# The first loads of a fused attention kernel: order of x and wkA, x's first chunk in two halves, the gate column, six warm-ups

## The chip, the cores and the metric

The kernel runs on one core of a Trainium2 chip. The metric is the device time of one execution in microseconds (us), measured over several executions; beside it there is one execution recorded by the hardware profiler, whose trace the profile lines in this document come from. TensorE (PE in the profile, with its weight loads as PEld) does the matrix products, VectorE (DVE) and ScalarE (ACT) the elementwise work, GpSimd (POOL) a few small copies. DMA transfers are issued from two queues, SyncE's (SP) and ScalarE's (ACT), and run on 16 shared DMA engines.

## The reference

Two linear-attention blocks, A and B, work on the same x (2048 rows of 640 values, bf16), with 32 heads of 20 values; a gate mixes their outputs row by row.

```python
g = sigmoid((x * gate_w).sum(-1, keepdims=True))
# for each of A and B:
q, k, v = split_heads(x @ wqkv)            # wqkv: 640 x 1920
phi = lambda t: where(t > 0, t + 1, exp(t)) + 1e-6
kv = einsum("bhsd,bhse->bhde", phi(k), v)
z = einsum("bhsd->bhd", phi(k))
num = einsum("bhqd,bhde->bhqe", phi(q), kv)
den = einsum("bhqd,bhd->bhq", phi(q), z)[..., None] + 1e-6
o = merge_heads(num / den) @ wo
out = g * o_A + (1 - g) * o_B
```

## The kernel before, in words

x is cut into 16 chunks of 128 rows, and the 640 features into 5 row blocks of 128 (DT = 5). A product with a weight needs x with features on the partitions (xT), while a load brings it with rows on the partitions (xn). For the first four chunks TensorE makes xT: `x_transpose` (L221) does five 128x128 transposes into PSUM, and VectorE copies them to xT, in two pieces where `cuts` says (0, 2, DT). The other twelve chunks are transposed on the way in by 15 DMA transposes on SP's queue (L137 to L141).

The program is one long TensorE stream. It begins with the warm-ups, matmuls on constants (L179), and the transposition of the gate vector into a column (L181 to L186): gate_w is loaded as a 5x128 tile `grow`, transposed by TensorE into the bank of the warm-ups, copied to `gsb` by VectorE, and written by five GpSimd copies into column 640 of wkA, one for each row block. The second half of every kA product is thus 321 columns wide (`k_mm`, L244), and its last column is the gate's logit.

Then `k_first` (L262) works through the first four chunks by hand, under a manual schedule, so that TensorE's order is the order of the code. Each chunk takes 10 matmuls, five row blocks by two halves of 320 columns, into one of four PSUM slots; the inner function `part(i, cs)` does the row blocks `cs` of chunk i. `k_done` (L251) hands a chunk to ACT (exp) and VectorE (two operations), which make phi(k). After it come the q blocks of the first 512 rows (`q_block`, L304), the other k chunks, and all later stages: the Gram products (`gs`, L380), the same for B, and the output stage. None of these is touched.

The loads of the first stage are issued in the order of the code, lines 125 to 141. Chunk q of the first 512 rows is made of the rows 4p + q, so that a load of one chunk (`load_x`) is 128 rows of 1,280 bytes; a row block of wkA (`load_wk`) is 128 rows of the same size. SP's queue issues x0, wkA's block 0, block 2, blocks 3 and 4 in one, then wqA in two loads, then the DMA transposes; ACT's queue issues the gate, x1, wkA's block 1, x2 and x3. Loads complete on eight semaphores taken in turn, so the ninth load waits, before it is issued, until the first has landed, and so on.

Of the kernel before, what the change touches and what calls it, by code (L numbers as in the profile page):

```python
# [8 lines left out]
P = 128  # L9
FP32 = mybir.dt.float32  # L10
BF16 = mybir.dt.bfloat16
# [3 lines left out]
S, D, H = 2048, 640, 32  # L15
Dh = D // H
DT = D // P
# [3 lines left out]
HB = 512  # L21
# [12 lines left out]
def kernel(  # L34
# [11 lines left out]
    nc = tc.nc  # L46
# [6 lines left out]
    work = ctx.enter_context(tc.tile_pool(name="work", bufs=2))  # L53
# [6 lines left out]
    def ps_raw(name, slot=None):  # L60

        if slot is None:
            slot = turn[0]
            turn[0] = (slot + 1) % 4
        return psum.tile([P, 4 * HB], BF16, tag=f"ps{slot}", name=name)

    def ps(name, slot=None):

        return ps_raw(name, slot).bitcast(FP32).rearrange("p (b n) -> p b n", b=2)

    xT = persist.tile([P, DT, S], BF16, name="xT")
    xn = persist.tile([P, ST, D], BF16, name="xn")
# [6 lines left out]
    ident = persist.tile([P, P], BF16, name="ident")  # L79
# [33 lines left out]
    xb0 = x2[0:CB * P, :].rearrange("(p q) d -> p q d", q=CB)  # L113
    wk = [None, None]
# [3 lines left out]
    def load_x(eng, lo, hi):  # L118
        eng.dma_start(out=xn[:, lo:hi, :], in_=xb0[:, lo:hi, :])

    def load_wk(eng, lo, hi):
        eng.dma_start(out=wk[0][:, lo:hi, 0:D], in_=wq_dram[0][:, lo:hi, D:2 * D])

    grow, logitT = R[0:DT, 0, 0, 0:P], R[0:2 * ST, 0, 1, 0:P]
    nc.scalar.dma_start(out=grow, in_=gate_w.rearrange("(c p) -> c p", p=P))
    load_x(nc.sync, 0, 1)
    load_x(nc.scalar, 1, 2)
    load_wk(nc.sync, 0, 1)
    load_wk(nc.scalar, 1, 2)
    load_wk(nc.sync, 2, 3)  # L130
    load_x(nc.scalar, 2, 3)
    load_wk(nc.sync, 3, DT)
    load_x(nc.scalar, 3, 4)
    wq[0] = wpool.tile([P, DT, D], BF16, tag="wq", name="wqA")
    for lo, hi in ((0, 2), (2, DT)):
        nc.sync.dma_start(out=wq[0][:, lo:hi, :], in_=wq_dram[0][:, lo:hi, 0:D])
    for n in range(1, NB):  # L137
        for c in range(DT):
            nc.sync.dma_start_transpose(
                out=xT[:, c, n * HB:(n + 1) * HB], in_=x2[n * HB:(n + 1) * HB, c * P:(c + 1) * P]  # L140
# [4 lines left out]
    for r in range(4):  # L145
        rows = slice(32 * r, 32 * r + 32)
        nc.gpsimd.tensor_copy(out=I4[rows], in_=ident[rows, rows])
    nc.gpsimd.tensor_copy(
        out=spread[:].rearrange("p (h t) -> p h t", t=TW), in_=I4[:, :, None].to_broadcast([P, H, TW])
    )  # L150
    nc.gpsimd.tensor_tensor(
        out=I16[0:2 * ST], in0=ident[0:2 * ST, 0:ST], in1=ident[0:2 * ST, ST:2 * ST], op=ALU.add
    )
    chosen = R[0:2 * ST, 1, 0:2, :].rearrange("p a (b n) -> p (a b) n", b=2)
    for h in range(2):
        for q in range(2):
            i0 = h * hc + q
            nc.gpsimd.tensor_copy(
                out=chosen[:, 2 * h + q, :].rearrange("p (j n) -> p j n", j=4),
                in_=I16[0:2 * ST, i0:i0 + hc - 1:2][:, :, None].to_broadcast([2 * ST, 4, 32]),  # L160
            )
    nc.gpsimd.memset(maskE[:], 1.0)
    for sign, base in ((1, 0), (-1, Dh - 1)):
        nc.gpsimd.affine_select(
            out=maskE[:], in_=maskE[:], pattern=[[-sign * Dh, WB[0] // Dh], [0, Dh]],
# [3 lines left out]
    for sign, base in ((1, 0), (-1, TW - 1)):  # L169
        nc.gpsimd.affine_select(  # L170
            out=headE[:], in_=headE[:], pattern=[[-sign * TW, H]],
# [4 lines left out]
    raw = ps_raw("warm", 3)  # L176
    warm = raw.bitcast(FP32).rearrange("p (b n) -> p b n", b=2)
    one_l, one_r = [nc.const_aps.tensor(1.0, [P, n], BF16) for n in (P, HB)]
    for k in range(7):  # L179
        nc.tensor.matmul(warm[:, 0, :], lhsT=one_l, rhs=one_r, start=True, stop=True)  # L180
    gcol = raw[:, 2 * HB:2 * HB + DT]  # L181
    nc.tensor.transpose(out=gcol, in_=grow, identity=ident[0:DT, 0:DT])
    gsb = work.tile([P, DT], BF16, tag="rT", name="gsb")
    nc.vector.tensor_copy(out=gsb[:], in_=gcol)
    for c in (0, 1, 2, 4, 3):
        nc.gpsimd.tensor_copy(out=wk[0][:, c, D:D + 1], in_=gsb[:, c:c + 1])  # L186

    def by_group(dst, lhsT, src, h):

        for c in range(DT):  # L190
            for j in range(4):
                r0 = h * 2 * HB + j * RB
                nc.tensor.matmul(
                    dst[32 * j:32 * j + 32, :], lhsT=lhsT[:, c, :], rhs=src[:, c, r0:r0 + RB],
                    start=(c == 0), stop=(c == DT - 1), tile_position=(0, 32 * j),
                )
# [24 lines left out]
    def x_transpose(i, slot, eng, cuts=(0, DT)):  # L221
        pt = ps_raw("xt", slot)
        for c in range(DT):
            nc.tensor.transpose(out=pt[:, c * P:(c + 1) * P], in_=xn[:, i, c * P:(c + 1) * P], identity=ident[:])
        copy = nc.scalar.copy if eng == "act" else nc.vector.tensor_copy
        src = pt[:, 0:D].rearrange("p (c n) -> p c n", c=DT)
        for lo, hi in zip(cuts, cuts[1:]):
            copy(out=xT[:, lo:hi, i * P:(i + 1) * P], in_=src[:, lo:hi])
# [15 lines left out]
    def k_mm(b, i, c, pt, hf):  # L244
        w = HF + (hf if b == 0 else 0)
        nc.tensor.matmul(  # L246
            pt[:, hf, 0:w], lhsT=xT[:, c, i * P:(i + 1) * P], rhs=wk[b][:, c, hf * HF:hf * HF + w],
            start=(c == 0), stop=(c == DT - 1),
        )

    def k_done(b, i, pt):  # L251
        side = (lambda: nc.scalar.copy(out=logit[:, i:i + 1], in_=pt[:, 1, HF:HF + 1])) if b == 0 else None
        phi(pk[:, i, :].rearrange("p (b n) -> p b n", b=2), pt[:, :, 0:HF], HF, side=side)

    def k_chunk(b, i, slot=None):
        pt = ps(f"k{'AB'[b]}", slot)
        for hf in range(2):
            for c in range(DT):
                k_mm(b, i, c, pt, hf)
        k_done(b, i, pt)  # L260

    def k_first():  # L262

        pts = [ps("kA", (2 + i) % 4) for i in (0, 1)]

        def part(i, cs):
            for c in cs:
                for hf in range(2):
                    k_mm(0, i, c, pts[i], hf)

        for i in range(2):
            x_transpose(i, i, "dve", (0, 2, DT))
        for i in range(2):
            part(i, (0, 1))
        for i in range(2):
            part(i, (2,))
        x_transpose(2, 0, "dve", (0, 2, DT))
        pts.append(ps("kA", 1))
        part(0, (3, 4))
        part(2, (0, 1, 2))  # L280
        x_transpose(3, 0, "dve")
        k_done(0, 0, pts[0])
        for i in (1, 2):
            part(i, (3, 4))
            k_done(0, i, pts[i])
        k_chunk(0, 3, 0)

    def mixed(t, m):

# [440 lines left out]
    with tc.manual_schedule():  # L730
        k_first()
# [9 lines left out]
    for n in range(1, NB):  # L741
        nc.sync.dma_start(
            out=xn[:, n * CB:(n + 1) * CB, :], in_=x2[n * HB:(n + 1) * HB, :].rearrange("(q p) d -> p q d", p=P)
# [8 lines left out]
    def bank(pool, name, n=1):  # L752
        return pool.tile([P, HB] if n == 1 else [P, n, HB], FP32, tag=name, name=name)

    with tc.manual_schedule():
# [31 lines left out]
        part = [slice(n * RB, (n + 1) * RB) for n in range(4)]  # L787
# [17 lines left out]
        with late_pool("single") as single:  # L805
# [6 lines left out]
            pts = [bank(single, f"s4{hf}")[:, 0:HF] for hf in range(2)]  # L812
# [76 lines left out]
```

## Time and profile before

| | us |
|---|---|
| median of 3 runs | 189.74 |
| lowest and highest | 189.58 and 189.91 |
| the profiled execution's own time | 189.64 |
| its span, first to last instruction | 187.9 |
| TensorE busy in the span | 183.5 |
| VectorE busy in the span | 149.9 |
| ScalarE busy in the span | 76.1 |

The profiled execution is longer than its span by 1.7 us, which lies before the first and after the last instruction. A line of the timeline gives the start and the length of a run of like instructions, the engine, the source line, the operation with what it writes and reads, the count, and in brackets the idle time of the engine before it and what ended that. A matmul's length includes its way through the array, so that neighbours overlap: 320 columns are listed with 299 ns, but start 136 ns apart. Engine names with a q are the sequencer's share, DMA issues above all; a DMA's landing is given as the time from its issue.

### The profile page before, as it was taken

What the parts mean: (1) busy time and instruction counts of PE and PEld (TensorE: products, weight loads), DVE (VectorE), ACT (ScalarE), POOL (GpSimd) and SP (SyncE); (2) the same over time, 40 slices, a digit from 0 to 9 for tenths busy, and PEclk for the clock granted to TensorE, in tenths of its full rate; (3) what the DMA queues carried; (4) which work ended last, traced back from release to release, by engine and by line L of the source; (5) the groups of instructions that cost most, each with busy time, mean ns of one, the idle gap of its engine ahead of it and who ended that gap; (6) DMA issues with size and microseconds to landing.
All of it is one profiled execution on the core that took longest, in us unless ns stands there. A gap on an engine that the chain in (4) does not pass through costs nothing.

```text
span 187.9 us, 3549 instructions
## 1 busy us (share of the span) xinstructions
PE 183.5 (98%) x1431; PEld 123.1 (66%) x1431; DVE 149.9 (80%) x246; ACT 76.1 (40%) x124; POOL 5.1 (3%) x29
## 2 busy tenths in 40 slices
PE   8999999999999999999999999999999999999993
PEld 3565757765567677877775555576778776777772
DVE  1387868889998998799888998739699989787453
ACT  2145545547952501267674577422401511111110
POOL 8100000010000000000000000000000000000000
PEclk9999999999999999999999999999999999999999
DMA  5985459962040000011115000000543003211222
GB/s 171 331 157 84 103 118 372 294 143 86 12 166 0 0 3 0 0 36 33 55 47 188 0 0 0 0 3 0 178 114 60 3 0 119 94 70 70 73 74 72
DMA packets 19173, 15.64 MB, mean 83 GB/s; under 512 B 8916, under 2 KB 19028, under 8 KB 19156
## 3 DMA queue, kind: packets, MB, share of 16 engines
q1 hardware_dynamic: 18282, 14.59, 27.7%
q10 hardware_dynamic: 874, 0.82, 1.4%
q8 instruction: 11, 0.18, 0.4%
q14 instruction: 6, 0.05, 0.1%
HBM read 10.00 MB, written 3.44 MB: 71 GB/s over the span
## 4 chain that ended last, share of the span: by engine, by line
PE 93%; DMA 3%; DVE 1%; SPq 1%; ACT 0%; issue 0%; DVEq 0%; ACTq 0%
PE gs L380 16%; PE kB L246 12%; PE qB L298 12%; PE kA L246 11%; PE ox L620 6%; PE qA L298 6%; PE oy L620 6%; PE oz L620 5%; PE qA L309 5%; DMA wkA<-in_A_wqkv_dram 3%; PE ow L620 3%; PE gA L353 2%; PE gB L353 2%; PE qA L319 1%; DVE osb L625 1%; PE mA L513 1%
## 5 line engine op out<-in xcount | busy, mean ns | idle before, releaser
L246 PEld LDWEIGHTS <-xT 128*128 128x128 bf16 x320 | 31.1, 98 | 12.6 <-issue 0.4
L246 PE MATMUL kB<-wkB,xT 128*128 128x320 bf16 x160 | 23.0, 299 | 0.0
L246 PE MATMUL kA<-wkA,xT 128*128 128x320 bf16 (+1 forms) x160 | 22.8, 299 | 0.1
L238 DVE TENSOR_SCALAR e<-e 128x640 bf16<-128x640 bf16 (+2 forms) x53 | 18.8, 355 | 5.0 <-ACT e L233 4.6
L298 PE MATMUL qB<-xT,wqB 128*128 128x512 bf16 x100 | 21.8, 379 | 0.0
L233 ACT ACTIVATE e<-kB 128x640 bf16<-128x640 f32 x16 | 11.3, 704 | 18.8 <-PE kB L246 17.5
L298 PEld LDWEIGHTS <-wqB 128*128 128x128 bf16 x100 | 11.7, 117 | 9.8 <-issue 0.2
L233 ACT ACTIVATE e<-kA 128x640 bf16<-128x640 f32 x16 | 11.2, 705 | 13.2 <-PE kA L246 13.2
L242 DVE SCALAR_TENSOR_TENSOR pk<-kA,e 128x640 bf16<-128x640 f32 x16 | 13.2, 824 | 2.5 <-PE kA L246 0.5
L242 DVE SCALAR_TENSOR_TENSOR pk<-kB,e 128x640 bf16<-128x640 f32 x16 | 13.2, 824 | 1.7
L233 ACT ACTIVATE e<-qB 128x1024 bf16<-128x1024 f32 x10 | 10.2, 1024 | 8.7 <-PE qB L298 7.2
L233 ACT ACTIVATE e<-qA 128x1024 bf16<-128x1024 f32 (+1 forms) x11 | 10.4, 946 | 8.1 <-PE qA L309 5.1
L664 ACT COPY u<-ox 128x320 f32<-128x320 f32 x8 | 3.4, 426 | 22.3 <-PE ox L620 22.3
L380 PEld LDWEIGHTS <-S 128*128 128x128 bf16 x96 | 9.4, 98 | 3.6
L380 PEld LDWEIGHTS <-xn 128*128 128x128 bf16 x96 | 9.1, 98 | 4.0 <-issue 0.4
L298 PE MATMUL qA<-xT,wqA 128*128 128x512 bf16 x50 | 11.0, 379 | 0.0
L620 PEld LDWEIGHTS <-xT 128*128 128x128 bf16 x85 | 8.0, 98 | 3.0 <-DVE xT L559 0.2
L648 ACT COPY p1s<-ox 128x320 f32<-128x320 f32 x8 | 3.4, 426 | 16.3 <-PE ox L620 16.3
L620 PEld LDWEIGHTS <-pqTB 128*128 128x128 bf16 x80 | 7.8, 98 | 3.1 <-issue 0.2
L620 PEld LDWEIGHTS <-pqTA 128*128 128x128 bf16 x85 | 7.9, 98 | 2.9 <-issue 0.2
L242 DVE SCALAR_TENSOR_TENSOR pqTB<-qB,e 128x1024 bf16<-128x1024 f32 x7 | 8.6, 1224 | 1.1 <-DVE e L238 0.5
L380 PE MATMUL gs<-pk,xn 128*128 128x320 bf16 x64 | 9.4, 300 | 0.0
(137 smaller groups left out, 290.9 us busy)
## 6 DMA issues: line engine op xcount, KB each, us to landing
out_dram<-osb SPq DMA_DIRECT2D x14, 160.0 KB, 1.8
xn<-in_A_x_dram SPq DMA_DIRECT2D x3, 640.0 KB, 6.3
wvA<-in_A_wqkv_dram SPq DMA_DIRECT2D x1, 800.0 KB, 9.9
wkB<-in_B_wqkv_dram SPq DMA_DIRECT2D x1, 800.0 KB, 4.5
wqB<-in_B_wqkv_dram SPq DMA_DIRECT2D x1, 800.0 KB, 4.5
MA<-ma_dram SPq DMA_DIRECT2D x1, 800.0 KB, 4.4
wvB<-in_B_wqkv_dram SPq DMA_DIRECT2D x1, 800.0 KB, 5.0
woB<-in_B_wo_dram SPq DMA_DIRECT2D x1, 800.0 KB, 5.7
```

The lines of the kernel that those rows point to most:

```text
L233: nc.scalar.activation(out=e[:], in_=src, func=ACT.Exp)
L238: nc.vector.tensor_scalar(e[:], e[:], 1.0, EPS, op0=ALU.min, op1=ALU.add)
L242: nc.vector.scalar_tensor_tensor(out=dst, in0=src, scalar=1.0 + EPS, in1=e[:], op0=ALU.add, op1=ALU.max)
L246: nc.tensor.matmul(pt[:, hf, 0:w], lhsT=xT[:, c, i * P:(i + 1) * P], rhs=wk[b][:, c, hf * HF:hf * HF + w], start=(c == 0), stop=(c == DT - 1),
L298: nc.tensor.matmul(pt[:, u, :], lhsT=mixed(wq[b][:, c, :], m), rhs=xT[:, c, n * HB:(n + 1) * HB], start=(c == 0), stop=(c == DT - 1),)
L309: nc.tensor.matmul(pt[:, u, :], lhsT=mixed(wq[b][:, c, :], m + u), rhs=xT[:, c, n * HB:(n + 1) * HB], start=(c == 0), stop=(c == DT - 1),)
L319: nc.tensor.matmul(pt[:, 0, :], lhsT=mixed(wq[b][:, c, :], m), rhs=xT[:, c, n * HB:(n + 1) * HB], start=(c == 0), stop=(c == DT - 1),)
L353: nc.tensor.matmul(pt[:, hf, 0:HF], lhsT=xn[:, i, c * P:(c + 1) * P], rhs=pk[:, i, hf * HF:(hf + 1) * HF], start=(i == 0), stop=(i == ST - 1),
L380: nc.tensor.matmul(pt[:, n, 0:HF], lhsT=left[:, i, n * P:(n + 1) * P], rhs=right[:, i, :], start=(first and i == 0), stop=(i == hc - 1), s ...
L620: nc.tensor.matmul(dst, lhsT=left[:, c, r0:r0 + P], rhs=right[:, c, :], start=(first and c == 0), stop=(c == DT - 1), skip_group_check=not ...
L648: nc.scalar.copy(out=self.p1s[:], in_=self.at("x"))
L664: nc.scalar.copy(out=self.u2[:], in_=self.at("x"))
```

## The change

The loads: x's chunk 0 goes in two halves of 64 partitions, one on SP and one on ACT, as the first load of each queue. The gate's load follows on ACT, then x1, x2 and x3. All of wkA is on SP: blocks 0, 1, 2, then 3 and 4. Chunks 2 and 3 of x are now asked for ahead of wkA's later blocks.

TensorE's order: six warm-ups, the transposes of chunk 0, then the gate column (now a function called between the transposes of chunk 0 and chunk 1), the transposes of chunk 1, row block 0 of both chunks, the transposes of chunk 2, row block 1 of chunks 0 and 1, blocks 0 and 1 of chunk 2, the transposes of chunk 3, block 2 of three chunks, and the rest. Chunk 3 is taken along in pieces, where before it was one `k_chunk` at the end. The number of matmuls and transposes, beyond the warm-up that goes, stays the same.

```diff
     grow, logitT = R[0:DT, 0, 0, 0:P], R[0:2 * ST, 0, 1, 0:P]
+    for eng, rows in ((nc.sync, slice(0, P // 2)), (nc.scalar, slice(P // 2, P))):
+        eng.dma_start(out=xn[rows, 0:1, :], in_=xb0[rows, 0:1, :])
     nc.scalar.dma_start(out=grow, in_=gate_w.rearrange("(c p) -> c p", p=P))
-    load_x(nc.sync, 0, 1)
     load_x(nc.scalar, 1, 2)
     load_wk(nc.sync, 0, 1)
-    load_wk(nc.scalar, 1, 2)
+    load_x(nc.scalar, 2, 3)
+    load_wk(nc.sync, 1, 2)
+    load_x(nc.scalar, 3, 4)
     load_wk(nc.sync, 2, 3)
-    load_x(nc.scalar, 2, 3)
     load_wk(nc.sync, 3, DT)
-    load_x(nc.scalar, 3, 4)
...
-    for k in range(7):
+    for k in range(6):
         nc.tensor.matmul(warm[:, 0, :], lhsT=one_l, rhs=one_r, start=True, stop=True)
-    gcol = raw[:, 2 * HB:2 * HB + DT]
-    nc.tensor.transpose(out=gcol, in_=grow, identity=ident[0:DT, 0:DT])
-    gsb = work.tile([P, DT], BF16, tag="rT", name="gsb")
-    nc.vector.tensor_copy(out=gsb[:], in_=gcol)
-    for c in (0, 1, 2, 4, 3):
-        nc.gpsimd.tensor_copy(out=wk[0][:, c, D:D + 1], in_=gsb[:, c:c + 1])
...
+    def gate_column():
+
+        gcol = raw[:, 2 * HB:2 * HB + DT]
+        nc.tensor.transpose(out=gcol, in_=grow, identity=ident[0:DT, 0:DT])
+        gsb = work.tile([P, DT], BF16, tag="rT", name="gsb")
+        nc.vector.tensor_copy(out=gsb[:], in_=gcol)
+        for c in range(DT):
+            nc.gpsimd.tensor_copy(out=wk[0][:, c, D:D + 1], in_=gsb[:, c:c + 1])
+
     def k_first():
...
+        x_transpose(0, 0, "dve", (0, 2, DT))
+        gate_column()
+        x_transpose(1, 1, "dve", (0, 2, DT))
+        pts = [ps("kA", (2 + i) % 4) for i in (0, 1)]
         for i in range(2):
-            x_transpose(i, i, "dve", (0, 2, DT))
+            part(i, (0,))
+        x_transpose(2, 0, "dve", (0, 2, DT))
         for i in range(2):
-            part(i, (0, 1))
-        for i in range(2):
+            part(i, (1,))
+        pts.append(ps("kA", 1))
+        part(2, (0, 1))
+        x_transpose(3, 0, "dve")
+        for i in range(3):
             part(i, (2,))
-        x_transpose(2, 0, "dve", (0, 2, DT))
-        pts.append(ps("kA", 1))
         part(0, (3, 4))
-        part(2, (0, 1, 2))
-        x_transpose(3, 0, "dve")
+        pts.append(ps("kA", 0))
+        part(3, (0, 1, 2))
         k_done(0, 0, pts[0])
-        for i in (1, 2):
+        for i in range(1, 4):
             part(i, (3, 4))
             k_done(0, i, pts[i])
-        k_chunk(0, 3, 0)
```

More of the change, by code (lines that the diff above doesn't have):

```diff
@@ L260, in k_chunk @@
         k_done(b, i, pt)
+    def gate_column():
[5 more added lines that the diff above has]
+            nc.gpsimd.tensor_copy(out=wk[0][:, c, D:D + 1], in_=gsb[:, c:c + 1])
     def k_first():
-        pts = [ps("kA", (2 + i) % 4) for i in (0, 1)]
         def part(i, cs):
```

## Prediction

> **What bounds the kernel now.** I read the page's busy row and slices first: is anything but TensorE the limit, and where is it not busy?
>
> ```profile
> span 187.9 us, 3549 instructions
> ...
> PE 183.5 (98%) x1431; PEld 123.1 (66%) x1431; DVE 149.9 (80%) x246; ACT 76.1 (40%) x124; POOL 5.1 (3%) x29
> ```
>
> TensorE is busy for 98%, and in the page's 40 slices only the first and the last are below nine tenths. The change touches only the first stage, so the second view is the chain of waits for the first 14 us.
>
> ```profile
> 2.19 5.70 DMA wkA<-in_A_wqkv_dram
> 7.89 0.04 issue
> 7.93 1.52 PE kA L246 x10
> 9.46 0.28 PE xt L224 x5
> 9.73 2.45 PE kA L246 x18
> 12.19 1.94 PE qA L309 x9
> ```
>
> The end of the program goes back, through TensorE alone, to a load of wkA (row blocks 3 and 4) that lands at 7.89. From 12.02, the first qA matmul's start, TensorE shows no wait of note until the tail: the windows from 12 to 164 us give it as busy throughout. So I take the time saved before 12.02 as the time saved at the end.
>
> The third view is TensorE's timeline in that stage (start, length, count, idle before it).
>
> ```profile
> 0.84 3.14 PE L180 MATMUL warm<-const-bfloat16-1.0 128*128 128x512 bf16 x7 [0.84 <-PEq L873]
> 3.92 0.18 PE L182 MATMUL warm<-ident,R 5*128 5x5 bf16 x1
> 4.03 1.11 PE L224 MATMUL xt<-ident,xn 128*128 128x128 bf16 x10
> 5.13 1.97 PE L246 MATMUL kA<-wkA,xT 128*128 128x320 bf16 x12
> 7.43 0.45 PE L224 MATMUL xt<-ident,xn 128*128 128x128 bf16 x5 [0.32 <-DMA xn<-in_A_x_dram]
> 7.93 1.52 PE L246 MATMUL kA<-wkA,xT 128*128 128x320 bf16 x10
> 9.29 0.44 PE L224 MATMUL xt<-ident,xn 128*128 128x128 bf16 x5
> 9.57 2.62 PE L246 MATMUL kA<-wkA,xT 128*128 128x320 bf16 x18
> ```
>
> By individual starts, three waits lose time: 0.17 for wkA block 1 (5.41 to 5.58), 0.49 for x's chunk 2 (6.94 to 7.43), 0.21 for wkA blocks 3 and 4 (7.72 to 7.93); 0.87 us in all. The clock is read off start-to-start times: 512 columns take 0.427 in the warm-ups and 0.216 in qA; the first transposes stand 0.107 apart, and from 4.87 on 0.056. TensorE is at half speed until about 4.8, though the granted-clock row shows 1.00.
>
> The fourth view is the landings, from the rows of x's and wkA's DMAs (issue plus time to landing), on two queues. SP: x0 0.81 to 3.07, wkA0 1.25 to 4.30, wkA2 1.72 to 5.34, wkA3-4 2.19 to 7.89. ACT: gate 0.80, x1 1.40 to 4.57, wkA1 1.80 to 5.54, x2 2.27 to 7.38, x3 at 2.77 (its landing is not recorded; by its packets about 8.3).
>
> ```profile
> L119 SPq DMA_DIRECT2D xn<-in_A_x_dram x1: 387/387/387, 0.8 to 0.8; - x1
> DMA to landing us min/median/max: 2.3/2.3/2.3
> ...
> L119 ACTq DMA_DIRECT2D xn<-in_A_x_dram x1: 370/370/370, 1.4 to 1.4; - x1
> DMA to landing us min/median/max: 3.2/3.2/3.2
> ...
> L119 ACTq DMA_DIRECT2D xn<-in_A_x_dram x1: 453/453/453, 2.3 to 2.3; - x1
> DMA to landing us min/median/max: 5.1/5.1/5.1
> ```
>
> In these last rows (x0, x1, x2) one sees that the queue is long: a transfer behind others takes 5.1 us where the first took 2.3. One 160 KB block occupies the engines about 0.45 us at the 370 GB/s of 8 us.
>
> **The change, part by part.** All working is against the profiled execution, 189.64 us, which is 0.10 under the median of the three runs.
>
> *DMA issues.* An issue of 64 rows is in no row; the bounds are 0.37 (a 128-row x issue on ACT) and 0.57 (the gate's 5 rows, 565 ns). I take 0.39, x0's own row. ACT then issues its half of x0 at 0.80, the gate at 1.23, x1 at 1.83 instead of 1.40, x2 at 2.24 and x3 at 2.74. SP issues its half at 0.81, wkA0 at 1.25, wkA1 at 1.72 (1.80 before, on ACT), wkA2 at 2.19. There are eight completion semaphores, so later issues wait for earlier landings: x3 for SP's half of x0 and wkA3-4 for ACT's half. Both halves together are the 160 KB that landed at 3.07, so wkA3-4 goes out at about 3.0 instead of 2.19. Behind it on SP are wqA's two loads (3.09 and 4.59 before; now after the gate's landing, about 3.5, and after wkA0's, about 4.3) and the x transposes by DMA (from 5.00). Nobody waits: wqA landed at 8.90 and 10.34 and is wanted from 11.46 and 11.9, the transposes are wanted at 17.6. Behind x3 on ACT is only the 1.28 us table load, 4 us ahead of its first use.
>
> *Warm-ups.* One of seven goes: 0.427 us, and x0's transposes start at 3.5 instead of 4.03. This I cost at nothing: x1's landing covers it. It would be worth up to 0.43 only if x1 had landed by 4.2.
>
> *Gate column.* Its transpose (0.11 us of TensorE) moves behind x0's, into the wait for x1: nothing. On DVE the copy gsb (0.16) now stands behind x0's two copies: these start at 4.3, gsb ends about 5.0, and POOL writes column 0 by 5.2 (row: 0.18 each, 0.12 apart) instead of 4.92. The first kA matmul that reads it comes at 5.2, so at most 0.1 us, and that beside the wait for x1's copy.
>
> *When x1 lands.* This price decides. The bounds are 4.30 (wkA0, second in line) and 5.54 (wkA1, fifth). By packet records, x1's first packets moved at 3.12, only when x0 and most of wkA0 were through, though it had been issued 1.4 us before; then wkA2 at 3.60 and wkA1 at 4.01. Its place, not its issue, set its landing. At 1.83 plus x0's 1.02 us from issue to first packet it is ready at 2.85, ahead of that slot. I take 4.70, next to the measured 4.57, with a quarter of the 0.43 later issue added.
>
> [...]
>
> *The TensorE path from there.* Load and first transpose 0.05 after landing, 4.75; four spacings (one or two of them at half speed) to the last start, 5.02; its end 0.22 later, 5.24; DVE's first copy 0.04 + 0.29, 5.57; chunk 1's first matmul 0.06 later, 5.63 (chunk 0's two fit before it), two of these at 0.136, 5.90. x2's transposes 0.28 + 0.05, 6.23, if x2 has landed by 5.9. Eight matmuls (block 1 of chunks 0 and 1; blocks 0 and 1 of chunk 2) 1.09, 7.32. x3's transposes 0.33, 7.65. The other 28 matmuls, 3.81: 11.46. Before, it was 12.02: 0.56 us saved.
>
> *What must land for that.* x2 by 5.9: it stands two blocks (0.9) behind x1, 5.6; bounds 5.54 and 7.38. wkA1 by 6.2 (5.54 before), x3 by 7.3 (two blocks more, 6.6 to 6.9), wkA2 by 7.65 (two blocks after wkA1, about 6.3), wkA3-4 by about 8.5: it is last of the same nine blocks that were in by 8.3, near 7.9. *After it:* chunk 0's phi ends at 9.12 + 0.03 + 0.70 (ACT) + 0.05 + 0.43 + 0.82 (DVE), about 11.2, and frees the PSUM slot of the first q block, 0.3 us before that needs it.
>
> Sum: 189.64 - 0.56 = 189.08, on the median's footing 189.2.
>
> **Rivals.**
> First: x1 misses its turn and moves fourth, behind wkA1, on at least one engine (the landing needs all sixteen). For it speaks that wkA1 is now issued first, by 0.1 us; against it the 0.25 us between 2.85 and 3.12. It costs one block, 0.45: end of the stage 11.91, a gain of 0.11 and 189.6, no change.
>
> Second, slower: the clock steps up later. TensorE now idles from about 4.2 to 4.75, just before the step at 4.8 that followed 4.0 us of unbroken work. If it stays at half speed until T, each us costs some 0.43. If the 4.0 us count anew from 4.75, T is 8.75: x1's transposes end at 5.5, the four first matmuls at 6.41 (0.27 each), x2's transposes at 6.99, block 1 at 8.07, three more slow matmuls, one fast, 9.02, x3's 9.35, 28 matmuls 13.16. That is 1.14 lost, 190.9. It eats the gain from T = 6.1 and is slower by 0.2% from about 7.0. Against it speaks that TensorE still works about 85% of the time up to 4.8; no row shows a step after a broken start.
>
> [...]
>
> Third: x2, asked for earlier, lands no earlier; some of x2's and x3's packets at 5.6 to 6.6 took 0.4 to 0.7 us instead of 0.055. From x2's landing the path is 5.61 long, so 7.38 ends it at 12.99: 190.7. It decides from 6.41.
>
> Fourth: the stage ends early, but the slot of chunk 0 or DVE's queue (four phis of 1.19 each) holds the q blocks up: 189.7.
>
> **How the numbers follow.** Forecast 0.40 (own range 188.9 to 189.4), x1 fourth 0.25, late clock 0.20, late x2 0.08, absorbed 0.07. 0.2% is 0.38 us, about what a measurement can tell. Faster by that: 0.36 of the forecast and 0.05 of x1 fourth (a gain between the two), 0.41; slower: late clock and late x2 with 0.01 each of x1 fourth and of absorbed, 0.30; the rest, 0.29. The range runs from 188.9 (x1 as early as 4.4) to 190.5 (T at 7.9); it cuts about half of the late clock, 0.10, the late x2, 0.08, and 0.02 below.
>
> **What would show it.** In the profile after: six warm-ups, x0's transposes near 3.5, the gate's transpose behind them, x1's landing near 4.7 with x1's transposes right after, no idle of TensorE between 5.9 and the first qA matmul, which starts near 11.5. x1 landing past 5.0 means the first rival; kA matmuls 0.27 apart after 5 us the second; idle before x2's transposes the third; an early last kA but a late first qA the fourth. The forecast is wrong if landings follow order of issue, or if the broken start costs the clock.

## The result and the profile after

The changed kernel is slower: a median of 191.22 us over 22 executions (189.70 to 193.72) against 189.64 us for the kernel before, also over 22 (188.95 to 191.01). The ratio is 1.0067, with a 95% interval of 1.0050 to 1.0084. The forecast was 189.2, with a range to 190.5. Every ratio in this document leaves out executions more than 1.5% above the fastest of their kernel: here five of the changed kernel, from 193.0 to 193.7 us, and none of the kernel before, so the loss is if anything understated.

One execution of the changed kernel was profiled first, and it happens to be the fastest of the 22, 189.70 us. The page's first lines:

```profile
span 188.0 us, 3552 instructions
...
PE 182.7 (97%) x1430; PEld 122.8 (65%) x1430; DVE 150.1 (80%) x246; ACT 76.0 (40%) x124; POOL 5.1 (3%) x29
```

TensorE's timeline of the first stage in this execution (start, length, count, idle before it):

```profile
0.84 2.72 PE L181 MATMUL warm<-const-bfloat16-1.0 128*128 128x512 bf16 x6 [0.84 <-PEq L879]
3.50 0.66 PE L218 MATMUL xt<-ident,xn 128*128 128x128 bf16 x5
4.09 0.17 PE L259 MATMUL warm<-ident,R 5*128 5x5 bf16 x1
5.38 0.45 PE L218 MATMUL xt<-ident,xn 128*128 128x128 bf16 x5 [1.11 <-DMA xn<-in_A_x_dram]
5.67 1.00 PE L240 MATMUL kA<-wkA,xT 128*128 128x320 bf16 x4
6.50 0.44 PE L218 MATMUL xt<-ident,xn 128*128 128x128 bf16 x5
6.78 1.27 PE L240 MATMUL kA<-wkA,xT 128*128 128x320 bf16 x8
8.23 0.45 PE L218 MATMUL xt<-ident,xn 128*128 128x128 bf16 x5 [0.18 <-DMA xn<-in_A_x_dram]
8.52 3.98 PE L240 MATMUL kA<-wkA,xT 128*128 128x320 bf16 x28
12.33 1.89 PE L315 MATMUL qA<-xT,wqA 128*128 128x512 bf16 x8
```

TensorE waits 1.11 us for x1, which lands at 5.33 and not at 4.70, and again for x3, which lands at 8.18. The first qA matmul starts at 12.33, 0.31 later than before, although this is the fastest of the 22. Most of them are slower. Another execution of the same, unaltered kernel, taken on another chip than the experiments below, took 191.71 us, longer than 16 of the 22, and its TensorE timeline is this:

```profile
0.84 2.72 PE L181 MATMUL warm<-const-bfloat16-1.0 128*128 128x512 bf16 x6 [0.84 <-PEq L879]
3.69 0.71 PE L218 MATMUL xt<-ident,xn 128*128 128x128 bf16 x5
4.34 0.18 PE L259 MATMUL warm<-ident,R 5*128 5x5 bf16 x1
6.56 0.72 PE L218 MATMUL xt<-ident,xn 128*128 128x128 bf16 x5 [2.04 <-DMA xn<-in_A_x_dram]
7.07 1.31 PE L240 MATMUL kA<-wkA,xT 128*128 128x320 bf16 x4
8.18 0.74 PE L218 MATMUL xt<-ident,xn 128*128 128x128 bf16 x5
8.71 1.74 PE L240 MATMUL kA<-wkA,xT 128*128 128x320 bf16 x8
10.29 0.44 PE L218 MATMUL xt<-ident,xn 128*128 128x128 bf16 x5
10.56 3.98 PE L240 MATMUL kA<-wkA,xT 128*128 128x320 bf16 x28
14.38 0.81 PE L315 MATMUL qA<-xT,wqA 128*128 128x512 bf16 x2
```

Two things differ. x1 is awaited for 2.04 us. And the same work takes longer: x1's and x2's transposes 0.72 and 0.74 where the one of 189.70 us has 0.45 and 0.44, the first eight-matmul block 1.74 where it has 1.27. TensorE runs at half speed until about 9.7 us, as it did in every traced execution up to 3.78 us or more. The stage ends at 14.38.

How x1 came to be so late is seen on ACT's queue. In the kernel before:

```profile
0.80 0.56 ACTq L125 DMA_DIRECT2D R<-in_gate_w_dram  x1
1.40 0.37 ACTq L119 DMA_DIRECT2D xn<-in_A_x_dram  x1
```

after the change, in the execution of 189.70 us:

```profile
0.81 0.55 ACTq L126 DMA_DIRECT2D xn<-in_A_x_dram  x1
1.39 0.77 ACTq L127 DMA_DIRECT2D R<-in_gate_w_dram  x1
2.19 1.35 ACTq L119 DMA_DIRECT2D xn<-in_A_x_dram  x3
```

and in the one of 191.71 us:

```profile
0.81 0.57 ACTq L126 DMA_DIRECT2D xn<-in_A_x_dram  x1
1.42 0.98 ACTq L127 DMA_DIRECT2D R<-in_gate_w_dram  x1
2.43 0.86 ACTq L119 DMA_DIRECT2D xn<-in_A_x_dram  x2
```

The issue of 64 rows takes 0.55 to 0.58 us, more than the 0.37 to 0.45 that loads of 128 rows took in the kernel before; the gate's issue behind it takes 0.77 or 0.98 where it took 0.56. So x1 is issued at 2.19 or 2.43 instead of 1.40.

### The profile page after: what moved, and what is told of

Same layout as the page of the kernel before. It is cut to its first block, busy times and chain, and to the rows that moved or that the text cites. A ratio compares the mean times of both kernels' runs of the same rounds, so it can differ in the third digit from the quotient of the medians.

```text
span 188.0 us, 3552 instructions
## 1 busy us (share of the span) xinstructions
PE 182.7 (97%) x1430; PEld 122.8 (65%) x1430; DVE 150.1 (80%) x246; ACT 76.0 (40%) x124; POOL 5.1 (3%) x29
## 4 chain that ended last, share of the span: by engine, by line
PE 92%; DMA 4%; DVE 2%; ACT 0%; issue 0%; DVEq 0%; ACTq 0%
PE gs L386 16%; PE kB L240 12%; PE qB L304 12%; PE kA L240 11%; PE ox L626 6%; PE qA L304 6%; PE oy L626 5%; PE oz L626 5%; PE qA L315 5%; DMA xn<-in_A_x_dram 4%; PE ow L626 3%; PE gA L359 2%; PE gB L359 2%; PE qA L325 1%; DVE osb L631 1%; PE mA L519 1%
## 5 line engine op out<-in xcount | busy, mean ns | idle before, releaser
L631 DVE TENSOR_TENSOR osb<-oz,u 128x320 bf16<-128x320 f32 (+1 forms) x18 | 8.0, 453 | 1.5 <-PE oz L626 0.8
```

The costliest lines, as they stand in the source:

```text
L631: nc.vector.tensor_tensor(out=dst, in0=acc, in1=sb, op=ALU.add)
```

## The experiments

Two theories stood at the start. By the late-landing theory the loss is what the landings of x make TensorE wait. By the late-clock theory the idle time that this opens keeps TensorE at half speed longer, and that is the larger part. Ratios are to the kernel before, run beside each on the same chip.

**The changed kernel again.**

> The changed kernel once more, unaltered, for a second trace. [...]

189.09 us, faster than any of the 22 (189.70 at best): x1 issued at 2.21 landed at 4.80, the spacing was 0.136 from 5.1 us on, and the first qA matmul started at 11.76. So the changed order can beat 12.02 when x1 is in time; this one said nothing of the slower executions.

**A fill behind the gate's transpose.**

```diff
         gate_column()
+        for k in range(3):
+            nc.tensor.matmul(warm[:, 0, :], lhsT=one_l, rhs=one_r, start=True, stop=True)
```

> The changed kernel with three more warm-up matmuls on constants between the gate's transpose and x1's transposes, where TensorE sat idle for 1.1 us. Their results are overwritten. Late-clock theory: the median falls from 191.2 to 189.8 to 190.2 us, and the spread of its executions shrinks to that of the kernel before (about 0.5 us for most). Late-landing theory: no gain, 191.2 us or up to 0.1 more, since no load is touched.

Median 190.90 (190.16 to 191.41), ratio 1.0075 (1.0056 to 1.0094). The median lies between the two expectations and decides nothing: the fill shares the gate's bank, so that it waited for VectorE's copy and started only at 5.12, after an idle 0.60, and x1 landed at 6.54 in the profiled execution (190.53 us), which left 0.66 more.

```profile
5.12 0.81 PE L275 MATMUL warm<-const-bfloat16-1.0 128*128 128x512 bf16 x3 [0.60 <-DVE gsb L261]
6.59 0.45 PE L218 MATMUL xt<-ident,xn 128*128 128x128 bf16 x5 [0.66 <-DMA xn<-in_A_x_dram]
...
13.19 3.18 PE L317 MATMUL qA<-xT,wqA 128*128 128x512 bf16 x14
```

The trace says more than the median. x1 landed as late as in the execution of 191.71 us (6.52), but the clock stepped up at 4.70 and stayed, and the first qA matmul started at 13.19 instead of 14.38. With x1's landing alike, that is 1.19 us for the clock, and the times differ by 1.18.

**Six warm-ups alone.**

```diff
-    for k in range(7):
+    for k in range(6):
```

> The kernel before with six warm-ups in place of seven, nothing else. TensorE then waits for x1 (4.57 us) for some 0.3 us after x0's transposes. [...] Late-landing theory: no change, 189.6 us, all executions alike.

Median 189.96, ratio 1.0003 (0.9977 to 1.0029), so the bulk is unchanged, as the late-landing theory expected; but 3 of its 12 executions, which the ratio leaves out, took 192.3 to 193.2, against 1 above 191 in 23 of the kernel before. One of the three was profiled: wkA1 landed at 7.08 there, TensorE idled 1.88 us, and then ran at half speed again from 7.71 to 11.12. So the kernel before can lose the clock behind a late landing, too. The warm-up that was removed is not the loss by itself; whether its removal makes such executions more frequent is not shown by 3 of 12 (the kernel before with x1 first on ACT, below, keeps all seven and has 3 of 12 above 191).

**x0 whole again, the gate first on ACT; everything else as changed.**

```diff
-    for eng, rows in ((nc.sync, slice(0, P // 2)), (nc.scalar, slice(P // 2, P))):
-        eng.dma_start(out=xn[rows, 0:1, :], in_=xb0[rows, 0:1, :])
     nc.scalar.dma_start(out=grow, in_=gate_w.rearrange("(c p) -> c p", p=P))
+    load_x(nc.sync, 0, 1)
     load_x(nc.scalar, 1, 2)
```

> The changed kernel with x's first chunk as one load on SP again and the gate's load ahead of x1 on ACT, as before; the rest as changed. Late-landing theory: the two queues' issues no longer hold each other up, x1 is issued near 1.4 and lands near 4.6 us instead of 5.3, and the median falls to about 189.2 us. Late-clock theory: the idle time before x1's transposes shrinks from 1.1 to about 0.4 us, so most executions step up in time: 189.2 to 189.8 us, with a tail of slow ones.

Median 189.30 (188.66 to 191.32), ratio 0.9998 (0.9975 to 1.0022). x1 was issued at 1.41 and landed at 4.17; x2 came at 6.45 and x3 at 8.16, and the first qA matmul started at 12.30. Undoing the halves alone takes the whole loss away. What is left of the change is worth nothing that the measurement can tell.

**Halves kept, the gate behind x1.**

```diff
-    nc.scalar.dma_start(out=grow, in_=gate_w.rearrange("(c p) -> c p", p=P))
     load_x(nc.scalar, 1, 2)
+    nc.scalar.dma_start(out=grow, in_=gate_w.rearrange("(c p) -> c p", p=P))
```

> The changed kernel with the gate's load behind x1's on ACT instead of ahead of it; the two halves of x0 stay on two queues. Issue theory (the halves, issued side by side, take 0.55 to 0.58 us each instead of 0.39, and the gate behind them 0.8 to 1.0, so that x1 goes out at 2.2 to 2.4 instead of 1.4): x1 goes out at about 1.4 and lands near 4.5, and the median falls to 189.2 to 189.5 us. Split theory (the halves themselves land slowly or upset the engines): no better than 190.5.

Median 191.56 (190.94 to 192.64), ratio 1.0086 (1.0052 to 1.0120): a miss for the issue theory. x1 was issued at 1.42 as expected, but that issue, too, now took 0.86 us, and the gate went out at 2.30; TensorE waited 1.10 us for the gate at 4.4 to 5.5, and the clock stepped up only at 9.7. x1 itself landed at 4.95. Whichever of the two stood behind the half on ACT, its issue was long: x1's 0.86 here, the gate's 0.77 or 0.98 in the order of the change.

**Both halves on SP.**

```diff
-    for eng, rows in ((nc.sync, slice(0, P // 2)), (nc.scalar, slice(P // 2, P))):
+    for eng, rows in ((nc.sync, slice(0, P // 2)), (nc.sync, slice(P // 2, P))):
```

> The changed kernel with both halves of x0 on SP, one after the other; ACT issues the gate first and x1 at about 1.4 us. Issue theory: two 64-row issues one after the other on a queue take about 0.4 us each, wkA0 goes out at 1.65, x1 is as early as in the kernel before, and the median is 189.3 to 189.6 us. Split theory: x0 lands past 3.5 us or x1 past 5, and the median stays above 190.3.

Median 191.71 (190.76 to 192.57), ratio 1.0080 (1.0052 to 1.0107): the split theory's outcome. SP's timeline begins so:

```profile
0.80 1.21 SPq L126 DMA_DIRECT2D xn<-in_A_x_dram  x2
2.06 1.53 SPq L122 DMA_DIRECT2D wkA<-in_A_wqkv_dram  x3
```

The two issues take 0.58 each although no other 64-row issue runs beside them, the second half lands at 4.40 and wkA0 at 6.59. So the price is of the 64-row issue itself, not of two of them at once. x1, on ACT, was early here (3.87) and it did not help: x0 itself was late, the first kA matmul waited for wkA0, and TensorE ran at half speed up to 11.67.

**The halves alone, in the kernel before.**

```diff
+    for eng, rows in ((nc.sync, slice(0, P // 2)), (nc.scalar, slice(P // 2, P))):
+        eng.dma_start(out=xn[rows, 0:1, :], in_=xb0[rows, 0:1, :])
     nc.scalar.dma_start(out=grow, in_=gate_w.rearrange("(c p) -> c p", p=P))
-    load_x(nc.sync, 0, 1)
```

> The kernel before with only x0's load changed: two halves on two queues, the gate behind the half on ACT, then x1, wkA1, x2, x3 as before; TensorE's order and seven warm-ups as before, so that TensorE now waits for the gate and then x1. Issue theory: x1 goes out at 2.2 and lands at 4.8 to 6.5, and the median rises by 0.5 to 1.6 us, to 190.1 to 191.2. Order theory (TensorE's new order is what is slow): unchanged, 189.6.

Median of 4 executions 192.55 (191.25 to 193.17), ratio 1.0127 (1.0082 to 1.0172). The old order of TensorE suffers at least as much as the new one: x1, issued at 2.43, landed at 6.30, TensorE idled 1.74 us, and ran at half speed from 7.72 to 11.14, as the transposes of 0.74 show.

```profile
6.35 0.45 PE L225 MATMUL xt<-ident,xn 128*128 128x128 bf16 x5 [1.74 <-DMA xn<-in_A_x_dram]
6.64 2.94 PE L247 MATMUL kA<-wkA,xT 128*128 128x320 bf16 x12
9.37 0.74 PE L225 MATMUL xt<-ident,xn 128*128 128x128 bf16 x5
```

The order theory falls; the size was underestimated by the clock's part.

**x0 whole on SP, x1 first on ACT, the gate second.**

```diff
-    for eng, rows in ((nc.sync, slice(0, P // 2)), (nc.scalar, slice(P // 2, P))):
-        eng.dma_start(out=xn[rows, 0:1, :], in_=xb0[rows, 0:1, :])
-    nc.scalar.dma_start(out=grow, in_=gate_w.rearrange("(c p) -> c p", p=P))
+    load_x(nc.sync, 0, 1)
     load_x(nc.scalar, 1, 2)
+    nc.scalar.dma_start(out=grow, in_=gate_w.rearrange("(c p) -> c p", p=P))
```

> The changed kernel with x0 as one load first on SP, x1 first on ACT at 0.8 us and the gate behind it. Issue theory: the two 128-row issues side by side take up to 0.7 us each, x0 and x1 both land by about 3.9, TensorE does not wait before x2, and the median is 188.8 to 189.3 us, under the kernel before. If x1's landing were not what the stage waits for, it stays at the 189.3 of the version with x0 whole and the gate first.

Median 189.43 (189.27 to 190.79), ratio 0.9975 (0.9953 to 0.9998): under the kernel before. It is 0.13 above what was expected, and not below the 189.30 of the version with x0 whole and the gate first; only the ratio is lower, because the kernel before took 190.14 beside this one and 189.63 beside that one. TensorE's timeline:

```profile
0.84 2.72 PE L180 MATMUL warm<-const-bfloat16-1.0 128*128 128x512 bf16 x6 [0.84 <-PEq L878]
3.68 0.71 PE L217 MATMUL xt<-ident,xn 128*128 128x128 bf16 x5
4.33 0.18 PE L258 MATMUL warm<-ident,R 5*128 5x5 bf16 x1
4.44 0.71 PE L217 MATMUL xt<-ident,xn 128*128 128x128 bf16 x5
4.95 1.38 PE L239 MATMUL kA<-wkA,xT 128*128 128x320 bf16 x4
6.12 0.74 PE L217 MATMUL xt<-ident,xn 128*128 128x128 bf16 x5
```

No wait for a landing stands between the warm-ups and x2's transposes. Two 128-row issues side by side take 0.39 and 0.42 us, where up to 0.7 was expected; x0 lands at 3.64 and x1 at 3.82. The clock steps up late even so (x2's transposes still take 0.74), but the stage ends at 11.89.

**Four more constant matmuls in the changed kernel, ahead of the gate's transpose.**

```diff
         x_transpose(0, 0, "dve", (0, 2, DT))
+        for k in range(4):
+            nc.tensor.matmul(warm[:, 0, :], lhsT=one_l, rhs=one_r, start=True, stop=True)
         gate_column()
```

> The changed kernel with four more matmuls on constants right after x0's transposes, ahead of the gate's transpose, so that TensorE works from 0.84 us to about 5.8 without a stop (the earlier fill waited for VectorE's copy of the gate and left a gap). Their results are overwritten; the gate column comes about 1.7 us later, which by itself holds the first kA matmul back to about 6.4 us. Late-clock theory: the step to full speed comes by about 7.4 us in every execution, none takes 193 us any more, and the median lies at 190.0 to 190.6. Landing theory alone (x1's landing sets the time, the clock nothing): no gain over 191.2, and the executions as far apart as before.

Median 190.03 (189.12 to 190.59), ratio 1.0006 (0.9985 to 1.0026). The late-clock theory's outcome: no load is touched, 1.9 us of useless work is added, and the median is that of the kernel before. In the timeline the fill stands where TensorE idled; x1's transposes behind it still run at half speed (0.64), and from the first kA matmul on all is at full speed:

```profile
4.07 1.91 PE L274 MATMUL warm<-const-bfloat16-1.0 128*128 128x512 bf16 x4
5.92 0.18 PE L259 MATMUL warm<-ident,R 5*128 5x5 bf16 x1
6.03 0.64 PE L218 MATMUL xt<-ident,xn 128*128 128x128 bf16 x5
6.51 1.00 PE L240 MATMUL kA<-wkA,xT 128*128 128x320 bf16 x4
7.38 0.45 PE L218 MATMUL xt<-ident,xn 128*128 128x128 bf16 x5
```

This run does not settle the matter alone. The unaltered changed kernel was not run beside it, and in this execution (190.20 us) the gate's issue took 0.78 and x1 landed at 5.04. With x1 at 6.54, full speed still gave 190.53 (the fill of three), so a median of 190.03 must have many early landings in it. How much of the gain is the clock's is not shown here; the next run shows the clock alone.

**Two warm-ups, with the good loads.**

```diff
-    for k in range(6):
+    for k in range(2):
```

> The version with x0 whole and x1 first on ACT, with two warm-ups instead of six: no load is touched, TensorE idles from 1.7 to 3.7 us and then meets the same landings. Late-clock theory: the step comes at 8 us or later and the median rises from 189.4 to 190.4 to 191.5 us. Landing theory: unchanged, 189.4 us, since TensorE waits for x at 3.7 us either way.

Median 190.56 (189.40 to 191.36), ratio 1.0027 (1.0002 to 1.0051); with seven, on the same chip, it was 189.50. In its timeline x0 and x1 are there in time, but the work up to 10 us is slow:

```profile
3.57 0.71 PE L217 MATMUL xt<-ident,xn 128*128 128x128 bf16 x5 [1.72 <-DMA xn<-in_A_x_dram]
...
6.63 0.72 PE L217 MATMUL xt<-ident,xn 128*128 128x128 bf16 x5 [0.42 <-DMA xn<-in_A_x_dram]
7.14 2.35 PE L239 MATMUL kA<-wkA,xT 128*128 128x320 bf16 x8
9.28 0.74 PE L217 MATMUL xt<-ident,xn 128*128 128x128 bf16 x5
```

The eight matmuls take 2.35 instead of 1.27. Idle time alone, with x0's and x1's landings early, costs about 1.1 us in the median (190.56 against 189.50).

**Seven warm-ups, with the good loads.** The edit is the same line, with 7.

> The version with x0 whole and x1 first on ACT, with seven warm-ups as in the kernel before: x0's transposes start about 0.25 us later, at 3.9, and TensorE works without a stop up to x2's landing near 6. Both theories: within 0.2 us of 189.4; the late-clock theory expects fewer slow executions than with six.

Median 189.50 (189.08 to 190.16), ratio 0.9976 (0.9958 to 0.9995), as expected. Six or seven makes no difference to the median; it is the second version that is faster than the kernel before, by 0.24%, with the same caution: the upper end of the interval is close to 1.

**x1 first on ACT in the kernel before.**

```diff
-    nc.scalar.dma_start(out=grow, in_=gate_w.rearrange("(c p) -> c p", p=P))
-    load_x(nc.sync, 0, 1)
+    load_x(nc.sync, 0, 1)
     load_x(nc.scalar, 1, 2)
+    nc.scalar.dma_start(out=grow, in_=gate_w.rearrange("(c p) -> c p", p=P))
```

> The kernel before with one exchange: x1 is issued first on ACT and the gate second. TensorE's order and seven warm-ups as before. Landing theory: x1 lands near 3.8 instead of 4.57, but in this order x1's transposes end before wkA0 and wkA1 have landed, and x2 still comes behind wkA1 on ACT: 189.4 to 189.7 us, so the gain of the version with x1 first also needs the changed order of x2, x3 and wkA. If the exchange alone makes the gain, 189.1 to 189.3 us.

Median 189.78 (189.26 to 192.15), ratio 1.0007 (0.9979 to 1.0036), within 0.1 of what the landing theory expected. The exchange alone shows no gain; the versions that gain have it together with the changed order.

**The unaltered changed kernel, three further executions.**

> The changed kernel unaltered, another trace. Late-clock theory: if the time is 190.3 us or more, a part of kA's first 40 matmuls or of the transposes runs at half speed (0.27 us and 0.107 us from start to start) after 7 us, and that accounts for 0.7 us or more. Landing theory: full speed throughout from 5.5 us on, and idle time before x1's or x2's transposes accounts for it.

> As the look before: late-clock theory, half speed after 7 us if the time is 190.3 us or more; landing theory, full speed and idle time.

> As the two looks before: late-clock theory, half speed after 7 us if the time is 190.3 us or more; landing theory, full speed and idle time.

191.71, 192.14 and 191.94 us. The kernel before took 192.47 in its one execution beside them, so this chip gives no loss to compare; what the three show is the mechanism. The first is the execution of 191.71 shown above. In all three the gate's issue took 0.98 to 1.00 us, x1 was issued at 2.43 to 2.44, behind wkA1 (2.06), and landed at 6.50 to 6.57. (The fill of three, on a chip where the kernel before took 189.63, has the same: 0.99, 2.43, 6.54.) And all three ran at half speed far past 7 us, up to 9.69, 11.17 and 9.85. In the second the clock had stepped up at 4.35 and was taken back, which the granted-clock column (PEclk) of the windows shows:

```profile
4.35:7.76 3.41, 1.10 (x11) 0.69 (x12) 1.03 (x5) 0.74 (x1) 1.07 (x8) 1.00 0.96 301
7.76:11.17 3.41, 3.41 (x21) 2.36 (x20) 0.70 (x3) 0.00 (x0) 0.00 (x0) 0.50 1.19 306
```

The columns are the stretch, its length, the busy time of PE, PEld, DVE, ACT and POOL, the granted clock, the DMA share and GB/s. In the 3.41 us up to 7.76 TensorE was busy for 1.10; for the next 3.41 it was granted half the clock, at the very time when it had all its work to do.

The same program steps up at 4 us in one execution and near 10 in another. What the traces show beside it is how busy TensorE was before each change of the clock. It is counted back here in stretches of 3.41 us, the length of the half speed from 7.76 to 11.17; that such stretches decide the clock is the author's reading, which fits the executions below but was not shown. In the five executions the stretch that ended with the step up was busy for 85% or more (85% up to 3.78 us, 92% up to 4.00, 98% up to 4.35, 92% up to 9.69 and to 9.85). In the last two the stretch before, up to 6.28 and 6.43, had only 45 and 40%, the wait for x1, and brought no step. At full speed, stretches with 64 and 74% kept it and the one with 32% lost it. TensorE does the same up to 3.4 us in all five, and yet the first step comes at 3.78, 4.00 and 4.35 in three of them and only at 9.69 and 9.85 in two; nothing in these traces sets that: this part is luck.

Both theories hold, in this proportion. The prediction's path (6.76 us from x1's landing to the first qA matmul, 5.61 from x2's, 4.19 from x3's, all at full speed) is set against what was measured, in the five executions of the changed kernel and in three of its versions:

| execution | x1, x2, x3 land | path at full speed ends | first qA matmul | difference, the clock's part |
|---|---|---|---|---|
| changed, 189.09 us | 4.80, 6.22, 6.76 | 11.83 (x2) | 11.76 | -0.07 |
| changed, 189.70 us | 5.33, 6.26, 8.18 | 12.37 (x3) | 12.33 | -0.04 |
| changed, 191.71 us | 6.52, 7.43, 8.37 | 13.28 (x1) | 14.38 | 1.10 |
| changed, 192.14 us | 6.50, 7.34, 8.25 | 13.26 (x1) | 14.79 | 1.53 |
| changed, 191.94 us | 6.57, 8.47, 9.48 | 14.08 (x2) | 14.62 | 0.54 |
| fill of three, 190.53 us | 6.54, 7.52, 8.55 | 13.30 (x1) | 13.19 | -0.11 |
| fill of four, 190.20 us | 5.04, 7.33, 8.13 | 12.94 (x2) | 12.87 | -0.07 |
| x1 first, two warm-ups, 191.36 us | 3.71, 6.59, 7.43 | 12.20 (x2) | 13.79 | 1.59 |

Against the 12.02 of the kernel before, the execution of 191.71 lost 1.26 us to landings and 1.10 to the clock. No traced execution of the unaltered kernel lies between 189.70 and 191.71, where 15 of the 22 do; a late x1 without a late clock, as in the fill of three, would put them there, but that is an inference. Three of the 22 (191.40, 191.53 and 191.85 us) have a mean granted clock of 0.991, like that of 192.14 (3.41 us at half speed are 0.9% of the 190), so the clock was very likely taken back in them, too.

## Why the prediction was wrong

*What bounds the kernel* held: time won or lost before the first qA matmul came out at the end nearly whole. The execution with 14.38 is 2.36 later at that point and 2.07 longer in time than the profiled execution before; the version with x1 first 0.13 earlier and 0.21 shorter. Up to 142 us the difference is carried along unchanged (2.35); the output stage then gives back 0.25 to 0.29 us in all five executions of the changed kernel, which is why that of 189.70 is 0.31 later at 12 us and only 0.06 longer.

*The DMA issues* were the step that failed. The prediction bounded a 64-row issue between 0.37 and 0.57 and took 0.39, x0's own row. It measured 0.55 to 0.58, the upper bound, and the gate behind it 0.77 to 1.00 where 0.57 was carried over. The term "x1 at 1.83 instead of 1.40" was therefore 2.19 or 2.43. That the issues behind it can grow was not considered at all; wkA0's on SP grew from 0.42 to 0.56 or 0.82. And x3 was put at 2.74, although the next sentences let it wait for half of x0 to land: it went out at 3.12 to 3.78, behind ACT's half.

*When x1 lands* failed with it. 4.70 was taken; 4.80 and 5.33 in the executions of 189.09 and 189.70 us, 6.50 to 6.57 in the slower ones. The argument that place and not issue sets the landing was wrong by half: place counts, but issue set the place. Issued at 2.19 to 2.21, ahead of wkA1 (2.30 to 2.32), x1 came before it, as the forecast said; issued at 2.43, behind wkA1 (2.06), it came after it. This is the first rival, whose price was far too low: not 0.45 but 1.2 to 1.8 us. One block's time is not what fourth place cost: x1 came 1.10 to 2.04 us behind wkA1 there. A pause of that kind is in the versions without halves, too: with x0 whole the landing after x1's 4.17 came at 6.24, with six warm-ups the one after 4.37 at 6.86, and in the kernel before the one after 5.54 at 7.38, where the prediction saw the slow packets. In third place x1 was ahead of it, in fourth behind it. The traces don't show what sets this order. Up to x2, the landings of the single blocks followed the order of issue in all five, but by the packet records, taken in each queue's order, the queues moved side by side: in the execution of 191.71 wkA1's packets started from 3.40 to 4.19 and x1's from 3.74 on.

*x0's halves* were not to land sooner, and the prediction did not count on it. They landed at 3.11 and 3.37 in the execution of 189.70 us, and the later one at 3.76 at worst, against 3.07 for the whole chunk. The split brought no earlier landing, and it cost at the issue as well: 0.55 to 0.58 us for a half, where the whole chunk took 0.39.

*The warm-up* at nothing was right for the bulk of the executions, as six alone show (1.0003). But its cover was x1's landing, and the idle time that is left there had a price of its own. The second rival named it: half speed until T, 0.43 us lost for each us. It was given 0.20. The three slower executions all have it, with 0.54 to 1.53 us; the two-warm-up version shows it with the loads held fixed, and the fill of three shows the time without it at the same landing of x1. Against it the prediction had said that TensorE would still work about 85% of the time up to 4.8: that was worked out from the idle time of a landing at 4.70, so the two errors were one. In the execution of 192.14 us the half speed that came back at 7.76 lasted 3.41 us, to 11.17.

*The TensorE path* was right: with the landings measured, its full-speed ends meet the four executions without a clock loss within 0.11 us. The third rival, x2 late, came true as well: in the execution of 191.94 x2 landed at 8.47, which ends the path at 14.08, where x1 alone would end it at 13.33. x3's landing, at 8.18 where 7.3 was asked, held the execution of 189.70 us. *The gate column, wqA, the DMA transposes and the PSUM slot* cost nothing in any trace of the changed kernel, as predicted.

So the changed order is not what loses. Nor does it bring the forecast's gain: its 11.46 for the first qA matmul was reached in no trace (11.76 and 11.83 at the best of this order), and in the trace with x0 whole and the gate first x1's early 4.17 was of no use, since x2 and x3 came late. Only with x0 whole and x1 first was it 0.24 to 0.25% faster, twice, by intervals that nearly reach 1. The loss is of the split, of what the queues behind it did to x1, and of the clock that the wait for x1 cost.

What stays open: why a 64-row issue takes longer than one of 128 rows; why the gate's issue takes 0.77 us in some executions and 0.98 in others (0.77 goes with 0.81 to 0.82 for wkA0 on SP, 0.98 with 0.56, so that what one queue gains the other loses, and x1 and wkA1 change places); and what makes the pause between the landings. The executions at 193 us were not caught in a trace; that they are the same causes at their worst is an inference. Their mean granted clock is 1.000, so it is not a clock taken back as in the execution of 192.14.

## What to carry to other kernels

A DMA issue is not priced by its bytes: a half of a load that is cut in two can hold its queue longer than the whole one (0.55 to 0.58 us for 80 KB, 0.39 for 160 KB here), and the price is paid by the transfer that stands behind it, first in its issue (the gate's 0.77 or 0.98 us against 0.56), then in its place among the others. Idle time of TensorE in the first microseconds can cost twice, once as a wait and once as half speed in the stretch that follows (1.26 and 1.10 us in the execution of 191.71 us), so a start-up stage is safer when the loads that it works on first are also issued first, or when filler keeps TensorE at work up to their landing. And one profiled execution can be the best of a wide spread: look at the spread before reading the trace as the kernel.

## What the runs showed of the hardware that was not expected

- A 64-row load of 80 KB took 0.54 to 0.58 us to issue, first or second on its queue, beside another 64-row issue or beside other issues; a 128-row load of 160 KB at the head of a queue took 0.39 to 0.42.
- The granted clock can fall back: a stretch of 3.41 us in which TensorE was busy for 1.10 us was followed by 3.41 us at 0.50, in the middle of dense work (the execution of 192.14 us). A stretch from 4.0 to 7.4 us with a 1.1 us wait in it, busy for 64%, was not (that of 189.70 us).
- Read off the spacing of the matmuls and the clock's record, the first step to full speed came at 3.78, 4.00, 4.35, 9.69 and 9.85 us in five executions of one program, and as late as 11.67 in a version of it. Counted back as above, over all traces, stretches of 3.41 us that ended with a step up were busy for 85% or more, those that brought none for 81% or less.
- By that reading, transposes would have to count as busy time: with x0 whole and x1 first, the stretch up to the step at 6.72 was busy for 96%, but for 55% without its transposes, while 72% of plain matmuls in the stretch before it had brought no step.
- Behind a 64-row issue, the gate's five-row load took 0.77 to 0.78 or 0.98 to 1.00 us to issue, never between; with the first x1 landed at 4.80 to 5.33, with the second at 6.30 to 6.57.
